# An attention and MLP kernel re-ordered by a list scheduler for all engines

## The chip, the cores and the metric

The kernel runs on one core of one Trainium2 chip. The metric is the device time of one execution in microseconds (us). Every kernel here was timed against the kernel before on the same chip, in turn; e1 to e4 ran on one chip, the later experiments on another, so experiments of different sets are best compared by their ratios to the kernel before. The profiled executions give a span, from the first to the last instruction, which is mostly about 1.7 us shorter than the time of the same execution. Executions are marked fast or slow; three slow ones (one of e1_hold, one of e7_resized, one of the kernel before in the rounds of e1 to e4) are left out of all ratios, but not out of the medians.

Engine names in the profile: PE is the matmul engine, PEld its weight load, DVE the vector engine, ACT the scalar engine, POOL is GpSimd, SP issues the DMAs.

## The reference

The program is the sum of a residual, a memory-augmented causal attention over four segments, and a SiLU MLP, all on one layer-normed input. S = 2048 rows, D = 512, 32 heads of 16, hidden size 1792, four segments of 512 rows.

```python
xn = layernorm(x)
# attention, per segment s and head
p     = softmax(qs @ ks.T * scale + causal_mask)
a_dot = p @ vs
a_mem = phi(qs) @ M / (phi(qs) @ z + 1e-6)
o     = g * a_mem + (1 - g) * a_dot
M, z  = M + phi(ks).T @ vs, z + phi(ks).sum()      # carried to the next segment
# sum
out = x + concat(o) @ wo + silu(xn @ w1) @ w2
```

## The kernel before

The heart of the kernel is a ring. Each segment has four blocks (dt) of eight heads, each block has five score tiles ("quads"), so there are 4 x 4 x 5 = 80 of them. A quad is a few matmuls into the PSUM tile `psS` (four banks, one buffer), one exp of 128x2048 elements on ACT into `Pt`, and a causal mask on POOL. There is one `psS`, so exp, next score matmul and next exp form a serial ring; I call the time from one exp's start to the next a turn. Everything else (projections q, k, v; the MLP's w1 and w2; the memory; normalisation; wo) is filled in between. It shares the other four PSUM banks, pool `pp`.

```python
ppool  = ctx.enter_context(tc.tile_pool(name="ppool", bufs=8))          # Pt
pp     = ctx.enter_context(tc.tile_pool(name="pp", bufs=4, space=PSUM)) # four banks
psatt  = ctx.enter_context(tc.tile_pool(name="psatt", bufs=1, space=PSUM))
ctx.enter_context(tc.manual_schedule(engines={ENG.PE}))   # only PE's order is the program's
...
def s_quad(st, dt, quad, tiles):
    psS = psatt.tile([P, 4, L], F32, name="psS")
    for par, kt, c in parts(quad):
        for g in range(4):
            nc.tensor.matmul(psS[:, g, c : c + nq], ...)   # four heads side by side
    Pt = ppool.tile([P, 4, L], BF16, name="Pt")
    nc.scalar.activation(out=Pt[:], in_=psS[:], func=AF.Exp, scale=SCALE)
    ...
    later(2000, masks)
```

PE's order comes from one loop: after each quad it fills about 1.5 us with generators (`due_fill`, `roll_fill`, `h_fill`), and at quad 1 of the next block it emits the block's PV, the product of the probabilities with V. PV makes two outputs, for even and odd heads, one bank each:

```python
if pend is not None and quad == 1:
    pv_part(*pend)
...
for par, dst in ((1, No_t), (0, N_t)):
    psPV = pp.tile([P, L], F32, name="psPV", tag="ps")     # one bank, filled and evacuated
    ...
```

The softmax sums of a segment are gathered by small DMAs into one tile `zf`, where ACT also writes the memory denominators; the tile is inverted, and spread again over 128 partitions by matmuls with a selection matrix. The output keeps one bank from the first w2 matmul to the last wo matmul:

```python
def replicate(ps, w, dt, rec):
    for b in range(2):
        nc.tensor.matmul(ps[:, 256*b : 256*b+256], lhsT=sel[:, b, w, dt, :], rhs=rec[:], ...)
...
w2_part(st, j, psO[:, :], ...)     # 14 matmuls, start at ft == 0
while st.get("normed", 0) < DT:    # the bank is held while normalisation is awaited
    yield
wo_part(s, st, j, psO[:, :], x_t)  # 4 matmuls, stop at the last
```

The softmax here doesn't subtract the row's maximum and nothing guards it: scores larger than these inputs give would overflow.

## Time and profile before

| | before |
|---|---|
| time, median of 5 runs (range) | 289.47 us (287.47 to 290.99) |
| profiled span | 288.9 us |
| first exp / last exp starts | 20.0 / 249.3 us |
| mean turn, (249.3 - 20.0) / 79 | 2.90 us |
| last exp's start to the end | 39.6 us |

Part 1 of the profile page of the kernel before gives, for each engine, busy time, share of the span and number of instructions.

```profile
span 288.9 us, 5119 instructions
PE 239.9 (83%) x1928; PEld 105.7 (37%) x1928; DVE 160.4 (56%) x280; ACT 203.0 (70%) x187; POOL 125.8 (44%) x222
```

No engine is full, so something serial must set the pace. The next view of the kernel before takes the exp's source line alone: count, shortest, median and longest duration in ns, first and last start, then what ACT sat idle for before it and who waited for it (us, times).

```profile
L484 ACT ACTIVATE Pt<-psS x80: 1856/1877/1933, 20.0 to 249.3; 128x2048 bf16<-128x2048 f32 x80
...
  PE psS L476: 19.3, 27
...
  PE psS L476: 21.0, 39
```

Eighty exps of 1.877 us are 150 us of a ring that lasts 231 us. The score matmul sometimes waits for the exp (21.0 us) and the exp sometimes for the score matmul (19.3 us): both sides of the ring are late in turn. The timeline of ACT in a quiet stretch of the kernel before shows how fast the ring can turn (start, duration, engine, line, operation, and in brackets the idle time before it with its releaser).

```profile
122.10 1.88 ACT L484 ACTIVATE Pt<-psS 128x2048 bf16<-128x2048 f32 x1
124.53 1.88 ACT L484 ACTIVATE Pt<-psS 128x2048 bf16<-128x2048 f32 x1 [0.56 <-PE psS L476]
127.14 1.88 ACT L484 ACTIVATE Pt<-psS 128x2048 bf16<-128x2048 f32 x1 [0.72 <-PE psS L476]
129.57 1.88 ACT L484 ACTIVATE Pt<-psS 128x2048 bf16<-128x2048 f32 x1 [0.56 <-PE psS L476]
```

These turns take 2.43 to 2.61 us, with 0.56 to 0.72 us of it the hand-over through PE. The mean of 2.90 us is therefore about 0.4 us above what the ring does when nothing is in its way. The end of the kernel before, in the timeline:

```profile
280.03 0.69 DVE L430 SCALAR_TENSOR_TENSOR o_t<-psO_3448,x_res 128x512 bf16<-128x512 f32 x1 [3.63 <-PE psO_3448 L424]
...
280.78 1.02 PE L424 MATMUL psO_3448<-wo_sb,oT 128*128 128x512 bf16 x4 [0.78 <-DVE o_t L430]
...
282.58 1.02 PE L424 MATMUL psO_3448<-wo_sb,oT 128*128 128x512 bf16 x4 [0.78 <-DVE o_t L430]
```

Each of the last three wo groups waits 0.78 us for the output operation of the group before it.

### The profile page before, as it was taken

To read this page: it belongs to the slowest core of one execution; us is meant where nothing else is said; L and a number is where in the kernel's file an instruction comes from. 1 tells how busy PE (TensorE), PEld (TensorE's weight loads), DVE (VectorE), ACT (ScalarE), POOL (GpSimd) and SP (SyncE) were. 2 spreads that over 40 slices of the span, in tenths; PEclk is the share of its full clock that TensorE was granted. 3 is DMA by queue.
4 is the path that set the end of the run, shared out by engine and by line. 5 is a ranking of instruction groups with operands and counts; after the bars stand their busy time and mean duration, and the time that the engine had idled before them with its cause. 6 is when DMAs were issued, how large, how long until landed. Compare 5 with 4: busy or idle time off the path is not lost.

```text
span 288.9 us, 5119 instructions
## 1 busy us (share of the span) xinstructions
PE 239.9 (83%) x1928; PEld 105.7 (37%) x1928; DVE 160.4 (56%) x280; ACT 203.0 (70%) x187; POOL 125.8 (44%) x222
## 2 busy tenths in 40 slices
PE   5277868877669885999998889699899999999983
PEld 5223324333223441334334343244353334444530
DVE  4439996666454746722157775652266533229722
ACT  1049868999938786877899789687768999714000
POOL 3807658566612468853334264844423334400000
PEclk9669979999989999899999999999999999999999
DMA  7998420101220011111201200001120010120003
GB/s 232 388 336 151 104 65 12 36 14 36 44 43 3 7 22 27 40 35 52 73 14 28 54 13 6 5 6 53 34 69 20 2 31 19 49 73 10 2 2 107
DMA packets 27065, 16.72 MB, mean 58 GB/s; under 512 B 15264, under 2 KB 26528, under 8 KB 27040
## 3 DMA queue, kind: packets, MB, share of 16 engines
q1 hardware_dynamic: 27040, 16.40, 21.0%
q8 instruction: 15, 0.25, 0.4%
q14 instruction: 10, 0.08, 0.1%
HBM read 9.96 MB, written 2.10 MB: 42 GB/s over the span
## 4 chain that ended last, share of the span: by engine, by line
PE 36%; ACT 23%; DVE 15%; issue 9%; DMA 7%; POOL 6%; SPq 2%; ACTq 0%; DVEq 0%
ACT Pt L484 18%; PE ps L188 12%; PE psO L415 7%; PE psS L476 4%; PE psO_3448 L415 4%; DMA xnT<-xn_t 3%; DMA x_in<-in_A_x_dram 2%; PE psO L424 2%; DVE qT L267 2%; ACT th L305 2%; POOL Pt L496 2%; DVE xn_t L143 2%; POOL ek L199 2%; DVE stats L132 2%; PE psPV L545 2%
## 5 line engine op out<-in xcount | busy, mean ns | idle before, releaser
L484 ACT ACTIVATE Pt<-psS 128x2048 bf16<-128x2048 f32 x80 | 150.2, 1877 | 21.9 <-PE psS L476 19.3
L496 POOL TENSOR_SCALAR_AFFINE_SELECT Pt<-Pt 128x512 bf16<-128x512 bf16 (+1 forms) x112 | 78.4, 714 | 103.0 <-ACT Pt L484 103.0
L188 PE MATMUL ps<-xnT,w_sb 128*128 128x512 bf16 x224 | 58.5, 392 | 4.9 <-DVE V_118 L273 2.3
L311 DVE SCALAR_TENSOR_TENSOR hT<-th,ps 128x512 bf16<-128x512 bf16 x56 | 37.8, 681 | 27.5 <-ACT th L305 27.1
L415 PE MATMUL psO<-w_sb,hT 128*128 128x512 bf16 x168 | 42.8, 386 | 0.0
L305 ACT ACTIVATE th<-ps 128x512 bf16<-128x512 f32 x56 | 33.5, 605 | 8.5 <-PE ps L188 5.1
L415 PEld LDWEIGHTS <-hT 128*128 128x128 bf16 x224 | 21.1, 99 | 24.8 <-issue 3.8
L476 PE MATMUL psS<-qT,kTo 32*128 32x512 bf16 (+3 forms) x256 | 17.7, 305 | 14.9 <-ACT Pt L484 13.5
L188 PEld LDWEIGHTS <-w_sb 128*128 128x128 bf16 x224 | 18.6, 99 | 30.8 <-issue 16.0
L476 PE MATMUL psS<-qT,kT 16*128 16x512 bf16 (+3 forms) x256 | 17.5, 302 | 7.7 <-ACT Pt L484 7.5
L430 DVE SCALAR_TENSOR_TENSOR o_t<-psO,x_res 128x512 bf16<-128x512 f32 x12 | 8.2, 687 | 27.5 <-PE psO L424 27.5
L476 PEld LDWEIGHTS <-kTo 32*128 32x128 bf16 x256 | 7.7, 92 | 34.9 <-issue 33.5
L199 POOL TENSOR_SCALAR ek<-ek 128x512 bf16<-128x512 bf16 x24 | 15.6, 650 | 7.9 <-ACT ek L196 7.8
L188 PE MATMUL ps<-xnT,wk_sb 128*128 128x512 bf16 x64 | 17.3, 395 | 1.4 <-DVE xn_t L143 0.7
L188 PE MATMUL ps<-xnT,wq_sb 128*128 128x512 bf16 x64 | 18.2, 411 | 0.0
L188 PE MATMUL ps<-wv_sb,xnT 128*128 128x512 bf16 x64 | 16.2, 390 | 1.3 <-DVE V_118 L273 1.2
L556 ACT CAST N_sb<-psPV 128x512 bf16<-128x512 f32 x16 | 9.4, 588 | 8.0 <-PE psPV L545 8.0
L132 DVE BATCH_NORM_STATS2 stats<-x_in 128x6 f32<-128x512 bf16 x16 | 10.4, 676 | 7.7 <-DMA x_in<-in_A_x_dram 7.7
L476 PEld LDWEIGHTS <-kT 16*128 16x128 bf16 x256 | 6.8, 92 | 20.7 <-issue 20.5
L267 DVE CAST qT<-ps 128x512 bf16<-128x512 f32 x16 | 11.0, 685 | 5.1 <-PE ps L188 5.1
L205 DVE SCALAR_TENSOR_TENSOR phiQT<-qT,ek 128x512 bf16<-128x512 bf16 x12 | 8.7, 724 | 9.0 <-POOL ek L199 9.0
L554 DVE CAST No_t<-psPV 128x512 bf16<-128x512 f32 x16 | 11.0, 687 | 4.7 <-PE psPV L545 4.7
(80 smaller groups left out, 273.1 us busy)
## 6 DMA issues: line engine op xcount, KB each, us to landing
w_sb<-in_B_w_dram SPq DMA_DIRECT2D x2, 1792.0 KB
x_in<-in_A_x_dram SPq DMA_DIRECT2D x8, 256.0 KB
x_res<-in_A_x_dram SPq DMA_DIRECT2D x16, 128.0 KB
out_dram<-o_t SPq DMA_DIRECT2D x16, 128.0 KB
N_sb<-No_t SPq DMA_DIRECT2D x64, 16.0 KB
wk_sb<-in_A_wk_dram SPq DMA_DIRECT2D x1, 512.0 KB
wq_sb<-in_A_wq_dram SPq DMA_DIRECT2D x1, 512.0 KB
wv_sb<-in_A_wv_dram SPq DMA_DIRECT2D x1, 512.0 KB
```

The costliest lines, as they stand in the source:

```text
L132: nc.vector.bn_stats(out=stats[:], in_=xts[(s, 2 * half + j)])
L188: nc.tensor.matmul(ps[:, :], lhsT=lhsTs(ki), rhs=rhss(ki), start=(ki == 0), stop=(ki == DT - 1))
L199: nc.gpsimd.tensor_scalar(out=ek[:], in0=ek[:], scalar1=1.0, scalar2=0.0, op0=ALU.min, op1=ALU.max)
L267: nc.vector.tensor_copy(out=st["qT"][:, dt, :], in_=ps[:, :])
L305: nc.scalar.activation(out=th[:], in_=ps[:, :], func=AF.Tanh, scale=0.5)
L311: nc.vector.scalar_tensor_tensor(out=hT[:], in0=th[:], scalar=1.0, in1=ps[:, :], op0=ALU.add, op1=ALU.mult)
L415: nc.tensor.matmul(psO, lhsT=st["hT"][ft][:, j * P : (j + 1) * P], rhs=w2_sb[:, ft, :], start=(ft == 0), stop=False,)
L476: nc.tensor.matmul(psS[:, g, c : c + nq], lhsT=kk[r0:r1, dt, kt * P : (kt + 1) * P], rhs=st["qT"][r0:r1, dt, kt * P : L], start=True, stop ...
L484: nc.scalar.activation(out=Pt[:], in_=psS[:], func=AF.Exp, scale=SCALE)
L496: nc.gpsimd.affine_select(out=v, in_=v, compare_op=ALU.is_ge, fill=0.0, base=0, pattern=[[0, v.shape[1]], [1, P]], channel_multiplier=-1,)
L554: nc.vector.tensor_copy(out=dst[:], in_=psPV[:, :])
L556: nc.scalar.copy(out=dst[:], in_=psPV[:, :])
```

## The change

The generators go. The whole program becomes a graph of operations, each with an engine, an occupancy and a latency in ns (a duration model), a due time, and the PSUM banks that it takes and frees. A greedy list scheduler orders all five instruction streams; the emission follows its order exactly, since every engine's order is now the program's. Along with it: x is loaded once and kept in SBUF; buffers become rings per block; the reciprocals are written to DRAM and read back replicated instead of being spread by matmuls; w2 and wo get separate accumulation groups with an SBUF partial sum `xa` between them; N casts, kT copies and the `zf` add move from ACT to DVE.

The diff, cut to its core:

```diff
-    ctx.enter_context(tc.manual_schedule(engines={ENG.PE}))
+    ctx.enter_context(tc.manual_schedule())
...
+RING = dict(xnT=2, kT=6, kTo=6, qT=6, ..., Pt=8, ..., rep=6, ..., psS=1, drec=4, ...)
+NB = 4
...
+            pvo = op("PE", 1090, 215, pv, tau(n0 + 8), r=keys + ..., w=[("PV", s, dt)],
+                     take=list(tk), mode="C", kind="PV")      # tk: TWO banks at once
...
+            op("DVE", 300, 130, norm, base + 2000 + 700 * j, ...)   # a duration of the model
...
-    def replicate(ps, w, dt, rec):      # matmuls with sel
+                def rep(K, dt=dt, w=w, slot=slot):
+                    d = K.drec[s][1 - w, 8 * dt : 8 * dt + 8, :]
+                    src = bass.AP(tensor=d.tensor, offset=d.offset, ap=[[L, 8], [0, 16], [1, L]])
+                    K.nc.sync.dma_start(out=K.rep[slot][:], in_=src)
...
+        split = True                    # w2 into xa, wo in a group of its own
...
+    def schedule(self):
+        while left:
+            best = None
+            for e in engs:
+                cand = None
+                for o in ready[e]:
+                    t = max(free[e], est[o.n])
+                    if o.take:
+                        av = sorted(b for b in banks)
+                        need = av[len(o.take) - 1]     # a PV needs the second-earliest bank
+                        t = max(t, need)
+                        if o.kind == "w1" and pend >= 2:
+                            t = INF
+                    ...
+                    slack = {"S": 110, "exp": 200}.get(o.kind, 0)
+                    key = -1e9 if o.kind in ("S",) else o.due
+                    ...
+                    if key < ck:
+                        if t - slack <= ct:            # urgent, but only if it starts as early
+                            cand = (t, key, slack, o)
+                    elif t < ct - cs:                  # else: the earlier start wins
+                        cand = (t, key, slack, o)
+                if cand and (best is None or cand[0] < best[0]):
+                    best = cand
```

## The prediction

> **What bounds it now.** The span is 288.9 us. No engine is full (page, part 1: PE 83%, ACT 70%, DVE 56%, POOL 44%), but a serial ring is long. The 80 exps of 128x2048 (80 x 1.88 us on ACT) share one PSUM tile, psS: exp, next score matmul, next exp. In the timeline its shortest turns are 2.41 to 2.61 us. The first exp starts at 20.0, the last at 249.3: 2.90 us a turn (by tens 3.1, 3.1, 3.4, 2.6, 2.8, 2.8, 2.8). The excess is order: in the waits view PE waits 21 us on exp for psS and ACT 19.3 us on score matmuls; the chain of waits at 100 to 120 us walks through POOL kTo and ek, DVE evacuations and ACT ek in turn. After the last exp 39 us follow: PV, seven left-over w1 groups, normalisation interleaved with w2, and four wo groups of which three wait 0.78 us for the output op before.
>
> PE's real occupancy: 512-column matmuls follow each other at 0.216 us. About 716 of them (155 us), 80 score quads at 0.43 (35), 16 PVs at 1.25 (20), rest 6: 216 us, after a first projection at 15.2 us. [...] 0.39 reported, 0.216 start to start.
>
> **What changes.**
> - Every engine's order, not PE's alone, comes from a list schedule, score matmuls first. This attacks the excess over about 2.5 us a turn: 79 x 0.35 to 0.45 = 28 to 36 us, on the critical path.
> - ACT loses 16 N casts (9.4), kT copies (2.3), zf (1.4): 13 us. DVE takes them, plus 16 w2 evacuations into xa (11): about 170 us, not binding.
> - 56 replication matmuls leave PE (6 us), and their tiles the four banks. In exchange a DRAM write and a replicated read, about 2 to 2.5 us each as the trace's small DMAs take; off the path except in the last segment. pq and a_t, reading SBUF only, should fall from 0.68 to about 0.4 us.
> - w2 apart from wo: no bank is held through normalisation; the last segment's w2 is done early.
> - x stays in SBUF: 16 reloads (2 MB) go; DMA was not binding.
>
> **Sum.** First exp stays near 20. 79 turns at 2.5 to 2.6 put the last at 218 to 226. Then a latency chain: mask and PV 2.5, evacuations 1.4, sums DMA 3.2, reciprocal 2, DRAM write and read 6.5, pq, psN, oT, four wo, output, store 10: about 26 us. Total 244 to 252, plus a little because a fixed order mis-times what the model mis-sizes: **251 us**, 8 in 10 within **241 to 267**. Chances: faster by over 2% 0.93, within 2% 0.04, slower 0.03.
>
> **What would show it.** Right: exps from about 20 to 222, mean turn below 2.65; ACT busy about 190; small PE waits on exp; last exp to end under 32 us, with DMA in its chain; wo four in a row. Wrong: turns still 2.8 or more, with ACT or PE waiting on DVE or POOL at the head of a fixed queue; x_all, one tile, serialising outputs against stores; a tail over 35 us from DMA hops.
>
> **What would make it wrong.** In-order engines block on an op the model put too early (DMA waits above all: zf sums, transposes, the DRAM hop), and one late op stops unrelated ones; SP's queue, about 0.5 us an issue, is in order too. POOL masks may come late for PV. If PE saturates, 216 us plus head and tail is the floor.

A last exp at 218 to 226 and a tail of about 26 us make 244 to 252, and 251 us was forecast. The DRAM write and read (2 to 2.5 us each, 6.5 in the sum) are an estimate from before's small DMAs: its chain of waits has 1.53 and 1.56 us for `zf` and 2.29 us for `N_sb`, after issues of 0.5 to 0.6 us; in after's tail the two took 5.81 us. `pq` and `a_t` took 0.68 us in before, with a PSUM operand, and a median of 0.42 us in after, from SBUF only.

## The result, and the profile after

| | before | after |
|---|---|---|
| time, median of 5 runs (range) | 289.47 us (287.47 to 290.99) | 277.84 us (275.94 to 278.57) |
| ratio of fast runs (95% interval) | 1 | 0.9599 (0.9539 to 0.966) |
| profiled span | 288.9 us | 274.2 us |
| first exp / last exp starts | 20.0 / 249.3 us | 14.15 / 244.46 us |
| mean turn | 2.90 us | 2.915 us |
| last exp's start to the end | 39.6 us | 29.7 us |

A ratio is the mean time of one kernel's fast runs over the mean of the other's fast runs of the same rounds, so it is not quite the ratio of the medians printed here.

The kernel is faster, but by 4%, not by the predicted 13%, and outside the range on record. The span fell by 14.7 us: 5.9 at the head, 9.9 in the tail, and the ring in between lasted 1.0 us longer than before (230.3 against 229.3). What the change was mainly for, the ring, gained nothing. These pieces are of one execution each. The one of after was the fastest of its five (275.94 us), which is why the spans differ by 14.7 us and the median times by 11.6.

Part 1 of the profile page after, in the same columns as before:

```profile
span 274.2 us, 4983 instructions
PE 228.6 (83%) x1857; PEld 97.7 (36%) x1888; DVE 177.2 (65%) x309; ACT 193.1 (70%) x164; POOL 124.0 (45%) x213
```

Work did move: ACT fell by 9.9 us (13 were costed), DVE rose by 16.8. The exp's line after (eight groups, since the ring has eight named buffers; two shown, then what ACT waited for before its exps and what the score matmuls waited for):

```profile
L488 ACT ACTIVATE Pt__129<-psS x10: 1858/1877/1878, 14.2 to 227.1; 128x2048 bf16<-128x2048 f32 x10
...
L488 ACT ACTIVATE Pt__136<-psS x10: 1877/1877/1907, 34.7 to 244.5; 128x2048 bf16<-128x2048 f32 x10
...
  PE psS L477: 29.5, 39
  PE psb__196 L515: 1.8, 1
  PE psb__194 L515: 1.7, 1
...
  PE psS L477: 9.5, 11
```

An exp lasts 1.877 us as before. PE now waits less for exps (9.5 us instead of 21.0) and ACT waits more for score matmuls (29.5 instead of 19.3). Two exps waited for a PV matmul (L515), which is new. Looking for the first of them in the timeline after:

```profile
28.45 1.09 POOL L502 TENSOR_SCALAR_AFFINE_SELECT Pt__133<-Pt__133 128x1024 bf16<-128x1024 bf16 x1
...
34.71 1.88 ACT L488 ACTIVATE Pt__136<-psS 128x2048 bf16<-128x2048 f32 x1 [1.04 <-PE psS L477]
...
37.61 1.02 PE L148 MATMUL psb__194<-xnT__89,w 128*128 128x512 bf16 x4
...
42.48 1.03 PE L148 MATMUL psb__197<-xnT__90,wq 128*128 128x512 bf16 x4
...
47.44 0.38 PE L148 MATMUL psb__195<-w,hT__137 128*128 128x512 bf16 x1
...
49.91 0.40 PE L515 MATMUL psb__194<-Pt__129,V__123 128*32 128x512 bf16 x4
...
50.36 1.88 ACT L488 ACTIVATE Pt__129<-psS 128x2048 bf16<-128x2048 f32 x1 [1.69 <-PE psb__194 L515]
```

Exp 7 (counting from 0) starts at 34.71 and exp 8 at 50.36: one turn of 15.65 us. Exp 8 writes `Pt__129`, the buffer of exp 0, which the PV of block 0 has to read first. The last input of that PV, the mask of `Pt__133`, was ready at 29.54, and yet the PV starts at 49.91. PE was idle for only 1.9 of these 20 us (1.52 of them in one wait that ended at 33.31): it ran w1, q, k, v and w2 groups. The bracket names only the last 1.69 us of idleness, because ACT had small work (tanh, exp for phi) before it; a reader who goes by the waits view alone misses this gap. The same stretch in windows of the kernel after (columns: stretch and its length; busy us and count of PE, PEld, DVE, ACT, POOL; granted TensorE clock; DMA share; GB/s):

```profile
20.00:35.00 15.00, 11.02 (x71) 3.85 (x70) 13.24 (x27) 11.02 (x11) 9.56 (x16) 1.00 0.69 126
35.00:50.00 15.00, 14.74 (x76) 6.28 (x79) 13.64 (x28) 10.41 (x18) 7.94 (x14) 1.00 0.18 36
50.00:120.00 70.00, 66.04 (x594) 28.45 (x604) 49.03 (x83) 62.75 (x56) 39.74 (x59) 1.00 0.18 35
```

PE and DVE look full in the stretch 35 to 50 (14.74 and 13.64 of 15 us), and ACT well used (10.41), although the ring stands still. PE does useful work there, but the wrong work.

The tail after, in the timeline:

```profile
254.11 0.35 DVE L641 TENSOR_SCALAR rec__173<-rec,gcol 128x256 bf16<-128x256 f32 x1
...
260.27 0.42 DVE L683 TENSOR_TENSOR pq__181<-phiQ__112,rep__176 128x512 bf16<-128x512 bf16 x1 [5.81 <-DMA rep__176<-drec__201]
260.75 0.58 PE L148 MATMUL psb__196<-pq__181,Mbf__190 128*128 128x512 bf16 x1 [12.10 <-DVE pq__181 L683]
...
265.75 0.63 PE L148 MATMUL psb__196<-wo,oT__166 128*128 128x512 bf16 x1
...
266.18 0.63 PE L148 MATMUL psb__196<-wo,oT__167 128*128 128x512 bf16 x1
...
268.90 0.38 PE L148 MATMUL psb__194<-wo,oT__166 128*128 128x512 bf16 x1
```

The tail is a latency chain now: from the reciprocals at 254.46 to the first product `pq` at 260.27 pass 5.81 us of DRAM write and read. PE waits 12.10 us, and its first back-to-back matmuls after that, from 265.75, follow each other at 0.43 us instead of 0.216; the granted clock was 0.50 from 253 to 265.37 and 0.52 from 265.37 to 268.7. The full rate is back at about 268.7 (granted clock 1.00 from there to 274), some 3.3 us after PE had come near to continuous work (265.37). The product `pq`, which now reads SBUF only, takes 0.42 to 0.43 us in this tail, where DVE's tensor-by-tensor operations with a PSUM operand take 0.67 to 0.69 in the same trace (`oT`), and `pq` itself took 0.68 in before, with a PSUM operand.

### The profile page after: what moved, and what is told of

Same layout as the page of the kernel before. It is cut to its first block, busy times and chain, and to the rows that moved or that the text cites. A ratio compares the mean times of both kernels' runs of the same rounds, so it can differ in the third digit from the quotient of the medians.

```text
span 274.2 us, 4983 instructions
## 1 busy us (share of the span) xinstructions
PE 228.6 (83%) x1857; PEld 97.7 (36%) x1888; DVE 177.2 (65%) x309; ACT 193.1 (70%) x164; POOL 124.0 (45%) x213
## 3 DMA queue, kind: packets, MB, share of 16 engines
HBM read 11.53 MB, written 2.33 MB: 51 GB/s over the span
## 4 chain that ended last, share of the span: by engine, by line
PE 47%; DVE 15%; ACT 13%; DMA 10%; issue 8%; SPq 4%; POOL 2%; DVEq 0%; ACTq 0%; POOLq 0%
PE psb__197 L148 11%; PE psb__195 L148 10%; PE psb__194 L148 8%; PE psb__196 L148 7%; PE psS L477 6%; ACT Pt__129 L488 3%; DMA wv<-in_A_wv_dram 3%; DMA x_all<-in_A_x_dram 2%; PE psb__196 L515 2%; ACT th__158 L434 1%; PE psb__197 L515 1%; ACT Pt__134 L488 1%; PE psb__194 L515 1%; DVE rec L640 1%; DMA rep__176<-drec__201 1%
## 5 line engine op out<-in xcount | busy, mean ns | idle before, releaser
L148 PEld LDWEIGHTS <-w 128*128 128x128 bf16 x224 | 21.4, 99 | 32.2 <-issue 11.5
L488 ACT ACTIVATE Pt__129<-psS 128x2048 bf16<-128x2048 f32 x10 | 18.8, 1875 | 6.7 <-PE psS L477 3.6
L488 ACT ACTIVATE Pt__134<-psS 128x2048 bf16<-128x2048 f32 x10 | 18.8, 1877 | 6.6 <-PE psS L477 4.6
L488 ACT ACTIVATE Pt__136<-psS 128x2048 bf16<-128x2048 f32 x10 | 18.8, 1880 | 5.8 <-PE psS L477 5.0
L488 ACT ACTIVATE Pt__133<-psS 128x2048 bf16<-128x2048 f32 x10 | 18.8, 1879 | 5.1 <-PE psS L477 4.2
L488 ACT ACTIVATE Pt__135<-psS 128x2048 bf16<-128x2048 f32 x10 | 18.8, 1875 | 3.7 <-PE psS L477 3.5
L488 ACT ACTIVATE Pt__131<-psS 128x2048 bf16<-128x2048 f32 x10 | 18.8, 1879 | 3.5 <-PE psS L477 3.3
L488 ACT ACTIVATE Pt__132<-psS 128x2048 bf16<-128x2048 f32 x10 | 18.8, 1877 | 3.2 <-PE psS L477 3.1
L488 ACT ACTIVATE Pt__130<-psS 128x2048 bf16<-128x2048 f32 x10 | 18.8, 1877 | 2.4 <-PE psS L477 2.2
L502 POOL TENSOR_SCALAR_AFFINE_SELECT Pt__129<-Pt__129 128x512 bf16<-128x512 bf16 (+1 forms) x14 | 10.7, 780 | 13.9 <-ACT Pt__129 L488 13.9
L502 POOL TENSOR_SCALAR_AFFINE_SELECT Pt__133<-Pt__133 128x512 bf16<-128x512 bf16 (+1 forms) x14 | 10.2, 746 | 11.9 <-ACT Pt__133 L488 11.9
L502 POOL TENSOR_SCALAR_AFFINE_SELECT Pt__136<-Pt__136 128x512 bf16<-128x512 bf16 (+1 forms) x14 | 9.6, 702 | 12.9 <-ACT Pt__136 L488 12.9
L502 POOL TENSOR_SCALAR_AFFINE_SELECT Pt__132<-Pt__132 128x512 bf16<-128x512 bf16 (+1 forms) x14 | 10.4, 759 | 10.7 <-ACT Pt__132 L488 10.7
L502 POOL TENSOR_SCALAR_AFFINE_SELECT Pt__135<-Pt__135 128x512 bf16<-128x512 bf16 (+1 forms) x14 | 10.0, 724 | 11.4 <-ACT Pt__135 L488 11.4
L502 POOL TENSOR_SCALAR_AFFINE_SELECT Pt__131<-Pt__131 128x512 bf16<-128x512 bf16 (+1 forms) x14 | 9.6, 701 | 10.4 <-ACT Pt__131 L488 10.4
L502 POOL TENSOR_SCALAR_AFFINE_SELECT Pt__134<-Pt__134 128x512 bf16<-128x512 bf16 (+1 forms) x14 | 9.8, 714 | 8.6 <-ACT Pt__134 L488 8.6
L502 POOL TENSOR_SCALAR_AFFINE_SELECT Pt__130<-Pt__130 128x512 bf16<-128x512 bf16 (+1 forms) x14 | 9.7, 707 | 8.5 <-ACT Pt__130 L488 8.5
L148 PE MATMUL psb__196<-xnT__89,w 128*128 128x512 bf16 x36 | 9.6, 379 | 4.0 <-DVE hT__139 L440 2.1
L148 PE MATMUL psb__196<-pq__181,Mbf__190 128*128 128x512 bf16 x2 | 1.2, 608 | 12.1 <-DVE pq__181 L683 12.1
L148 PEld LDWEIGHTS <-wk 128*128 128x128 bf16 x80 | 7.4, 98 | 10.5 <-issue 3.6
L148 PEld LDWEIGHTS <-wq 128*128 128x128 bf16 x80 | 7.2, 97 | 9.6 <-issue 2.7
L148 PE MATMUL psb__194<-xnT__90,w 128*128 128x512 bf16 x36 | 10.3, 408 | 0.0
```

The lines of the kernel that those rows point to most:

```text
L148: K.nc.tensor.matmul(K.bank(t)[:, 0:ncol], lhsT=lhsT(K, i), rhs=rhs(K, i), start=(i == 0), stop=(i == n - 1),)
L488: K.nc.scalar.activation(out=K.Pt[n % RING["Pt"]][:], in_=K.psS[:], func=AF.Exp, scale=SCALE)
L502: K.nc.gpsimd.affine_select(out=a, in_=a, compare_op=ALU.is_ge, fill=0.0, base=0, pattern=[[0, a.shape[1]], [1, P]], channel_multiplier=-1,)
```

## The experiments

My theory (A) was starvation by bank count. PV asks for two banks at one moment, all other groups for one. The scheduler takes the operation that can start earliest, and a more urgent one displaces it only if it can start as early. With four banks in constant use, the second-earliest free bank always comes after the earliest, so a one-bank group always starts earlier than PV. PV waits until the one-bank work runs dry, and with it the ring, which has only eight `Pt` buffers for blocks of five. The scheduler writes its planned start times down, and they can be read without a chip: planned exp 7 and 8 are at 30.0 and 46.3 us, and the first PV, whose inputs the plan has ready at 26.1, is placed at 45.0. So the gap is in the plan, and the chip carried it out. The plan's span is 262.2 us, the chip's 274.2. (The schedule was computed again, without a chip. If the test lets a PV start when one bank is free, exp 8 is planned at 32.5 us. If instead a rule that is cut from the diff above goes, which delays a PV by 0.7 us before its due time, exp 8 stays at 46.3. So in the plan it is the test for two banks that makes the gap.)

The rivals were that the moved work slows the ring (DVE's load, the DRAM hop, w2 apart from wo), and that the fixed order of in-order engines does so, by blocking on operations that the model mis-times. The expectations below name the theories by letters; each states its own, and A is the same throughout the first five runs.

| kernel | first exp | last exp | mean turn | last exp to end | span | time, median | ratio to before (95%) |
|---|---|---|---|---|---|---|---|
| before | 20.0 | 249.3 | 2.90 | 39.6 | 288.9 | 289.47 | 1 |
| after | 14.15 | 244.46 | 2.915 | 29.7 | 274.2 | 277.84 | 0.9599 (0.9539, 0.966) |
| e1_hold | 13.96 | 224.57 | 2.666 | 31.0 | 255.6 | 257.19 | 0.8847 (0.8766, 0.8928) |
| e2_joint | 13.96 | 256.11 | 3.065 | 41.4 | 297.5 | 300.05 | 1.0372 (1.0279, 1.0464) |
| e3_joint_hold | 14.24 | 228.10 | 2.707 | 46.9 | 275.0 | 278.83 | 0.9616 (0.952, 0.9712) |
| e4_tailpe | 14.10 | 229.28 | 2.724 | 29.0 | 258.3 | 258.55 | 0.8917 (0.8838, 0.8996) |
| e5_peonly | 23.42 | 273.05 | 3.160 | 30.4 | 303.5 | 306.04 | 1.0536 (1.0484, 1.0588) |
| b1_late_x | 17.49 | 249.03 | 2.931 | 39.6 | 288.6 | 290.3 | 1.0007 (0.9976, 1.0038) |
| e6_lesspe | 14.37 | 223.27 | 2.644 | 29.6 | 252.9 | 256.06 | 0.8824 (0.8789, 0.886) |
| e7_resized | 16.63 | 219.97 | 2.574 | 32.0 | 252.0 | 253.44 | 0.8717 (0.8668, 0.8767) |
| e8_vlate | 13.29 | 219.36 | 2.608 | 31.0 | 250.4 | 252.31 | 0.872 (0.8685, 0.8755) |
| e9_vlate_tailpe | 13.40 | 218.91 | 2.601 | 27.9 | 246.8 | 248.5 | 0.8582 (0.8553, 0.861) |
| e10_tuned | 13.35 | 222.09 | 2.642 | 27.7 | 249.8 | 251.56 | 0.8688 (0.866, 0.8716) |

Starts and turns are read from the traces, in us. All results matched the reference within its tolerance, e6_lesspe too, which is wrong, so this check did not see the matmuls left out.

### e1_hold: banks are held for a PV that is due

When a PV is ready and due, another operation may take a bank only if that leaves two for the PV, that is, if three are free by then (`av` is the sorted list of the times at which the banks come free).

```diff
                         if o.kind == "w1" and pend >= 2:
                             t = INF
+                        if o.kind != "PV" and t < INF:
+                            due_pv = [x for x in ready["PE"] if x.kind == "PV" and est[x.n] <= t and x.due <= t]
+                            if due_pv and av[2] > t:
+                                t = INF
```

> The one edit: while an overdue PV block waits for its two PSUM banks, no other group may take a bank if that would leave fewer than two. Theory A (the list schedule starves PV of two banks at once; the stall of exp 7 to 8, 15.6 us in the trace, is written into the order itself): the stall shrinks to under 7 us, the last exp comes near 226 instead of 244.5, the time near 260 us (256 to 264). Rival B (PE was busy with needed work during the stall, so the work only moves): the stall goes but the other turns lengthen; time 273 to 279 us. Rival C (the in-order engines mis-time, whatever the order says): the time falls by less than half of the 18 us by which the plan's own end falls (262.2 to 244.0).

Measured: 257.19 us (255.22 to 259.25), 20.6 us less than after. The timeline of e1_hold at the same place:

```profile
34.17 1.88 ACT L488 ACTIVATE Pt__136<-psS 128x2048 bf16<-128x2048 f32 x1 [1.04 <-PE psS L477]
...
37.66 0.40 PE L515 MATMUL psb__196<-Pt__129,V__123 128*32 128x512 bf16 x4 [0.41 <-DVE hT__143 L440]
...
38.64 1.88 ACT L488 ACTIVATE Pt__129<-psS 128x2048 bf16<-128x2048 f32 x1
```

The turn from exp 7 to exp 8 fell from 15.65 to 4.47 us. That is 11.2 of the 19.7 us that the ring lost; the remaining 8.5 are spread over the other 78 turns (2.75 to 2.64 us on average). The plans fit this: in the plan of after, six of the later PVs stand 4 to 9 us behind their inputs (for example placed at 139.0, ready at 129.9) and all stand behind their due times; in the plan of e1_hold no PV after the third is more than about 3 us behind its inputs. A part of the 8.5 may be the TensorE clock: in after it was granted at 0.50 from 215 to 220 us and 0.65 from 220 to 226, while over its whole ring e1_hold had 0.99; what this cost was not measured. Theory A is confirmed. Its rivals are refuted as the main cause: B expected 273 to 279 us and C a fall of less than half of 18 us, and with the moved work and the fixed order of engines unchanged in kind the time fell by 20.6 us and the ring turns in 2.666 us.

### e2_joint and e3_joint_hold: w2 and wo in one group again, without and with the hold

```diff
-        split = True
+        split = False
```

> Undoes one part of the change: w2 and wo of a token block are again one accumulation group of 18 matmuls in one bank (the flag for it is in the code), nothing else. Theory A (banks decide): a group of 18 that waits for normalisation holds a bank much longer, PV starves more, plan 281.2 instead of 262.2; the time is 290 to 300 us, with a stall before exp 8 near 21 us and another near exp 53. Rival B (PE's work decides): 16 output evacuations less on DVE and the same PE work; time 273 to 282 us.

> The joint w2 and wo group together with the bank hold of the first run of this set. Theory A: plan 260.8; time 272 to 280 us, stall before exp 8 below 7 us; splitting w2 from wo is then worth 14 to 20 us by itself, mostly at the end (last exp as in the first run, the tail longer by about 15 us since w2 of the last segment sits behind normalisation or holds all banks). Rival B: same as the first run of this set within 5 us.

Measured: e2_joint 300.05 us, e3_joint_hold 278.83. The joint group holds a bank through normalisation, which makes the second bank rarer. In e2_joint the stall before exp 8 grew, as the timeline of ACT shows:

```profile
33.86 1.88 ACT L488 ACTIVATE Pt__136<-psS 128x2048 bf16<-128x2048 f32 x1 [1.04 <-PE psS L477]
55.26 1.86 ACT L488 ACTIVATE Pt__129<-psS 128x2048 bf16<-128x2048 f32 x1
```

That is 21.4 us for one turn. So w2 apart from wo did not cause the stall, it eased it. With the hold, the difference between split and joint is 278.83 - 257.19 = 21.6 us, a little over what I had expected. Most of it lies in the tail, 46.9 against 31.0 us after the last exp. In e3_joint_hold PE waits 12.17 us, until 248.95, and runs w2 of the last segment only from 254.12; in e1_hold, where w2 keeps no bank, it starts at 224.39, before that segment is normalised.

### e4_tailpe: the DRAM hop of the last segment undone, on top of e1_hold

```diff
+        onpe = s == NSEG - 1
+        if not onpe:
             op("SP", 1500 if s else 500, 2100, wr, ...)         # write of rec to DRAM
+        if onpe:                                                # two matmuls per tile instead
+            K.nc.tensor.matmul(K.bank(tk)[:, 256*b : 256*b+256],
+                               lhsT=K.sel[:, w, b, dt, :], rhs=K.rec[i2][:], ...)
```

> Bank hold as in the first run, and in the last segment alone the reciprocals are replicated by selection matmuls on PE as before the change, not through DRAM. Theory D (the DRAM hop costs the tail): from the reciprocal's end to the first pq the trace showed 5.8 us of DVE waiting; matmuls need about 1; last exp to end falls from about 30 to 24 to 26 us, time 3 to 6 us under the first run. Rival E (the tail is bound by the chain of DVE, PE and output after it, and PSUM operands make pq and a_t 0.68 instead of 0.42 us): within 2 us of the first run.

Measured: 258.55 us, 1.4 us more than e1_hold, with overlapping intervals of the ratio, so no difference is shown. The run is confounded, because adding operations makes the greedy scheduler choose another order everywhere: the last exp came at 229.28 instead of 224.57. In the tail itself the way from the start of the reciprocal to the end of the last `oT` fell from 14.8 to 10.5 us, but the reciprocal began 5.2 us after the start of the last evacuation (239.22 against 234.06) where e1_hold took 3.6 (232.92 against 229.34), queued behind an `xa` operation on DVE that waited 2.33 us for PE. And from 248.13 to 253.56 its wo matmuls followed each other at 0.43 us, with the granted clock at 0.50. So the hop cost about 4.3 us where it stood, and the experiment didn't show whether removing it pays. That was tried again in e9_vlate_tailpe.

### e5_peonly: after's PE program, the other engines' order left to the framework

As in the kernel before, only PE's order is the program's. PE's program is identical to that of after.

```diff
-    ctx.enter_context(tc.manual_schedule())
+    ctx.enter_context(tc.manual_schedule(engines={mybir.EngineType.PE}))
```

> The changed kernel with the planned order kept on PE alone; the other engines are ordered by the framework, as in the kernel before. PE's program is the same, 182 rows of DVE's, some 40 of ACT's and 30 of POOL's move. Theory A (the changed kernel's time is set by PE's order, with its starved PV, and not by the order of the other engines): 275 to 282 us, stall before exp 8 still 14 to 17 us. Rival F (the order of all engines is what gave the 4%): 286 us or more, first exp back near 20.

Measured: 306.04 us, 28 us more than after and 5% more than before. My expectation was wrong: I had thought the stall alone made the time and the order of the other engines worth little. The first cost is at the head, in the timeline of e5_peonly:

```profile
15.35 0.69 DVE L277 BATCH_NORM_STATS2 stats__85<-x_all 128x6 f32<-128x512 bf16 x1 [5.79 <-DMA x_all<-in_A_x_dram]
15.96 0.67 DVE L322 CAST xnT__89<-psb__196 128x512 bf16<-128x512 f32 x1
...
16.78 1.86 PE L148 MATMUL psb__195<-xnT__89,wk 128*128 128x512 bf16 x4 [5.67 <-DMA bcol<-in_A_beta_dram]
```

DVE has the statistics of segment 1 at the head of its queue and waits 5.79 us for their load, while the evacuation of segment 0's transposed x, which PE needs, stands behind them. (The releaser named for PE is only the last of several; what PE needed is the cast just before it.) The first exp comes at 23.4 instead of 14.15, the stall at exp 8 is still there (43.52 to 59.20), and the mean turn is 3.16 us. So the planned order of the other engines is worth 28 us with this PE program, which was planned together with it; what it is worth with another PE program this doesn't say. The kernel before carries a similar wait (4.18 us of DVE on a load at 10.59); I asked next whether it costs anything there. The converse, a program's order for DVE or for all engines in the kernel before, could not be built for all engines: with the emission order taken literally, the check before the chip reports a deadlock. So that corner stays untested.

### b1_late_x: the kernel before, with segment 1's first load behind the weights

```diff
-    load_x(1, 0)
     for dst, src in ((w1_sb, B_w1), (wo_sb, A_wo), (w2_sb, B_w2)):
         nc.sync.dma_start(out=dst[:], in_=src.rearrange("(ko ki) n -> ki ko n", ki=P))
+    load_x(1, 0)
     load_x(1, 1)
```

> The kernel before with one load moved: the first half of x of segment 1 is loaded after w1, wo and w2, so that its statistics no longer stand in DVE's queue ahead of the first normalisations. Theory G (the 5.9 us by which the first exp came earlier after the change is this head-of-queue wait of DVE, 4.2 us in the trace, plus POOL memsets ahead of the first power): first exp at 16 to 18.5 instead of 20.0, and the time 1 to 4 us under before. Rival H (the head was gained by something else: x ring, fewer loads): first exp stays at 19.5 to 20.5.

Measured: 290.3 us, ratio 1.0007: the same time. The first exp did move, from 20.0 to 17.49. By exp 10 the gain was gone (52.55, against 51.06 in before). The head is not on the path of the kernel before: the exps that follow wait for other things. My expectation was right about the first exp and wrong about the time.

### e6_lesspe: e1_hold with 48 matmuls of w2 left out (wrong)

```diff
+                if name == "w2" and i in (3, 7, 11):
+                    return
```

> Wrong result on purpose: the bank-hold version in its exact order, but 3 of the 14 w2 matmuls of each token block are not emitted: 48 matmuls of 0.216 us, 10.4 us of PE. Theory I (once the stall is gone PE is the bound: 18 to 20 of 20 us busy in most stretches): 7 to 10 us under the bank-hold version (257.2), so 247 to 250. Rival J (the ring of exp and score matmul, or order, sets the pace): under 4 us, so 253 to 258.

Measured: 256.06 us, 1.1 us less than e1_hold, for 48 x 0.216 = 10.4 us less PE work. The two were run on different chips, and the intervals of their ratios overlap. PE is 90% busy on the page of e1_hold, and taking this work from it gained next to nothing. That fits rival J, ring or order; the run doesn't tell these two apart. The prediction's floor ("If PE saturates, 216 us plus head and tail is the floor") is none: with the head and tail of e1_hold it would be 216 + 14.0 + 31.0 = 261 us, and e1_hold's span is 255.6, since some of PE's work lies in the head and the tail.

### e7_resized: e1_hold with durations taken from the trace

I compared start-to-start times on DVE and POOL in the trace with the model's occupancies, and set the ones that were off to their measured means.

```diff
-            op("DVE", 662, 150, stats, ...      ->  805
-            op("POOL", 770, 150, rstd, ...      ->  960
-            op("DVE", 300, 130, norm, ...       ->  490
-            op("POOL", 655, 130, odd, ...       ->  750
-        op("DVE", 690 if acc else 605, 140, st  ->  790 / 705
-                op("DVE", 340, 135, a0, ...     ->  560
-            op("DVE", 340, 135, pq / at, ...    ->  435 / 460
-        op("DVE", 1900, 150, rc, ...            ->  2070
```

> The bank-hold version planned with DVE and POOL durations as the trace has them (statistics 0.81 instead of 0.66, normalisation 0.49 for 0.30, pq and a_t 0.44 to 0.46 for 0.34, phi 0.10 more, reciprocal 2.07 for 1.90, POOL kTo and power longer). Plan 247.1 instead of 244.0. Theory C (the 11.6 us between plan and trace in the bank-hold run are order gone wrong through mis-sized ops): trace minus plan falls to 7 or less and the time to 250 to 255. Rival K (the difference is work and clock that no order removes): 256 to 261.

Measured: 253.44 us, 3.7 us less than e1_hold, on another chip; the intervals of the two ratios just touch (0.8766 and 0.8767), so the gain is likely but small. The mean turn is 2.574, inside the predicted 2.5 to 2.6, in part by luck: the first exp came 2.7 us later than in e1_hold, which shortens the ring, and with the first exp back the mean turn is 2.608 (e8_vlate). The plan is now 4.9 us short of the chip (247.1 against 252.0) instead of 11.6 in e1_hold (244.0 against 255.6). Part of what the model missed is not the operation's own time. The layer-norm scaling has, in the view of its source line in after:

```profile
L296 DVE TENSOR_SCALAR xn__88<-x_all,mv,rstd x8: 394/400/1240, 7.2 to 132.0; 128x512 bf16<-128x512 bf16 x8
```

Its median is 0.40 us and its longest 1.24 us; that longest one, in the timeline of after, started in the same moment as a POOL mask that ran for 1.09 us:

```profile
28.45 1.24 DVE L296 TENSOR_SCALAR xn__88<-x_all,mv,rstd 128x512 bf16<-128x512 bf16 x1
28.45 1.09 POOL L502 TENSOR_SCALAR_AFFINE_SELECT Pt__133<-Pt__133 128x1024 bf16<-128x1024 bf16 x1
```

This is a coincidence of two operations, and another one went differently: the same operation at 48.60 began while POOL was at work (48.27 to 48.88, as far as POOL's times can be trusted) and took 0.42 us. No run here tests whether POOL's work is what lengthens DVE's. A duration model with one number per operation can hold the mean of this and not the case.

### e8_vlate, e9_vlate_tailpe, e10_tuned: towards the best version

In e7_resized the first exp had slipped from 13.96 to 16.63, because a v group of segment 0 was placed ahead of the first k and q. e8_vlate lets v groups of segment 0 start no earlier than 13 us in the plan. e9_vlate_tailpe adds e4's edit for the last segment. e10_tuned changes two of the scheduler's constants.

```diff
 e8:  +            nb=13000 if s == 0 else 0,        # not_before of the first v matmul
 e9:  + e4's edit, the selection matrix built after 60 us
 e10: -T0 = 12500                                     +T0 = 11500
      -slack = {"S": 110, "exp": 200}                 +slack = {"S": 160, "exp": 200}
```

> The resized version with one more edit: the V projections of segment 0 may not start before 13 us, since in the resized run they stood ahead of the first k and q and the first exp came at 16.6 instead of 14.0. Plan 247.2 (resized 247.1). Theory L (the head is on the path once the rest flows): first exp at 14.0 to 14.6 and the time 1 to 3 us under the resized version (253.4). Rival M (as in the kernel before, where a first exp 2.5 us earlier gained nothing): 252.5 to 255.

> The previous kernel of this set plus the last segment's reciprocals replicated by matmuls instead of through DRAM; unlike in the first try the order before the tail is kept (same planned start of the last exp, 212.4; plan 242.7 against 247.2). Theory D2 (the first try lost in the middle what it saved in the tail): time 3.5 to 5.5 us under the previous kernel; last exp at the same time within 0.7 us; last exp to end 26 to 28 us instead of 31. Rival E: within 1.5 us of it.

> The previous kernel with two numbers of the scheduler changed after trying 160 combinations on the plan alone (origin of the due dates 11.5 us instead of 12.5, slack by which a score matmul may jump the queue 160 ns instead of 110). Plan 239.7 against 242.7. If the plan's differences of 3 us are real on the chip: 2 to 4 us under the previous kernel, 243 to 247 us. If they are within what the plan cannot see (trace minus plan was 4.9 to 11.6): no different, 246 to 251.

Measured: 252.31, 248.5 (248.22 to 249.18) and 251.56 us. e8_vlate moved the first exp by 3.3 us (13.29) and left the ratio as it was (0.872 against 0.8717); at exp 10 the two kernels stand at 42.76 and 42.82. The head isn't on the path here either. e9_vlate_tailpe gained 3.8 us over e8_vlate with its last exp at nearly the same time (218.91 against 219.36); 27.9 us are left after it instead of 31.0. Here the experiment of e4 is clean, and leaving out the DRAM hop of the last segment is worth 3 to 4 us. With the hop, in e8_vlate, wo ran at 0.43 us a matmul from 242.12 to about 244.3, and the mean granted clock was 0.986 against 0.998 in e9_vlate_tailpe; how much of the gain this makes was not measured. The tail of e9_vlate_tailpe in the timeline:

```profile
230.19 0.35 DVE L656 TENSOR_SCALAR rec__174<-rec,gcol 128x256 bf16<-128x256 f32 x1
...
232.34 0.69 DVE L711 TENSOR_TENSOR pq__182<-phiQ__113,psb__198 128x512 bf16<-128x512 bf16 x1 [0.82 <-PE psb__198 L683]
...
240.26 0.39 PE L148 MATMUL psb__198<-wo,oT__170 128*128 128x512 bf16 x1 [0.99 <-DVE oT__170 L733]
240.48 0.38 PE L148 MATMUL psb__197<-wo,oT__167 128*128 128x512 bf16 x1
```

`pq` starts 1.8 us after the reciprocals, not 5.81, though it reads PSUM and takes 0.69 us. PE has w2 work left until then and never idles for more than 0.99 us, and wo runs at 0.216 us from its start. e10_tuned had the shortest plan of all (239.7 us, against 242.7 for e9) and ran 3 us longer than e9: a difference of 3 us between these two plans said nothing about the chip. e9_vlate_tailpe is the best kernel, 14% below before and 11% below after.

## Why the prediction was wrong

The step that failed is, as it was put, "79 turns at 2.5 to 2.6 put the last at 218 to 226". The ring took 230.3 us where 79 x 2.55 = 201 us were expected. The other two terms, "First exp stays near 20" and a tail of "about 26 us", were off by -5.9 and +3.7, so the ring's +28.9 us is more than the whole miss of 26.8 (277.84 against 251); that the other two terms cancel in part is luck. What failed is the assumption that the scheduler's order keeps every turn near 2.5: it let PV, which needs two banks, starve, and one turn alone took 15.65 us. The runs account for most of it: banks held for PV took the ring from 230.3 to 210.6 us (e1_hold). Measured durations took it to 203.3 (e7_resized), of which 2.7 us is only the later first exp; the last exp moved by 4.6 (224.57 to 219.97). With the first exp back the ring is 206.1 us (e8_vlate), 4.6 above the expected figure, and these are not explained.

- "Every engine's order, not PE's alone, comes from a list schedule, score matmuls first. This attacks the excess": right that order is the matter (e5_peonly: 28 us for the order of the other engines, with this PE program). Wrong that this scheduler's order has no excess of its own. Its text was in the diff: PV takes two banks, and a one-bank operation with an earlier start beats a more urgent one. I priced the operations and did not follow the choice rule through one block.
- "plus a little because a fixed order mis-times what the model mis-sizes": the mechanism fits, and was worth about 3.7 us in time (e7_resized, with intervals that just touch). It was the smaller of the two.
- "Wrong: turns still 2.8 or more, with ACT or PE waiting on DVE or POOL at the head of a fixed queue": the turns were 2.915, but for another reason. ACT waited for a PV that PE had been given no banks for, and PE was busy almost all the while.
- "First exp stays near 20": it came at 14.15; an earlier first exp was worth nothing in the two kernels where it was tried alone (b1_late_x, e8_vlate), and in after itself it was not tried.
- The tail, "about 26 us": measured 29.7, with the DRAM hop in its chain and the wo groups in a row, as described. Matmuls at 0.43 us instead of 0.216, after a wait of 12.10 us, add to it.
- ACT's loss ("13 us", "ACT busy about 190") and DVE's gain ("about 170 us, not binding") were roughly right: 193.1 us, a loss of 9.9, and 177.2. The SBUF-only products (`pq`, `a_t`) fell from 0.68 to a median of 0.42 us (0.41 to 1.22), as costed. `x_all` as one tile did not serialise stores and outputs: the waits view of after names no store as what an output operation waited for.
- "PE's real occupancy" by 0.216 us a matmul was useful in showing that PE had room; e6_lesspe fits it.
- "w2 apart from wo: no bank is held through normalisation; the last segment's w2 is done early": right, and worth more than I had expected in e3_joint_hold (14 to 20): 21.6 us with the hold (e3_joint_hold against e1_hold), and 22.2 without it (e2_joint against after), there with a longer stall in it.

What stays open: how much a program's order for all engines would give the kernel before with its own PE order (it could not be built), why single DVE operations took 1.24 and 1.64 us where 0.40 and about 0.68 are common, and how the 11.6 us that the change did gain divide among its parts; only w2 apart from wo was undone by itself.

## What to carry to other kernels

When a program is ordered by a greedy scheduler, an operation that needs two of a scarce resource at once can starve behind those that need one, unless something is held back for it; follow the choice rule through one round of the critical ring, or look at the planned starts for the longest gap, before pricing operations. A gap in the ring can hide behind busy engines, so plot the spacing of the ring's own instruction rather than waits or busy shares. And before crediting a gain at the head, see whether a later step of the ring (exp 10 here) still has it.

## What the runs show of busy shares, the clock and DVE beside POOL

- Busy shares: ACT was 70% busy in after and PE 83%. But the same operations in another order gained 20.6 us (e1_hold) with ACT's work as it was (193.1 and 192.2 us), and 10.4 us less work on PE gained 1.1 us (e6_lesspe). The shares did not point to what the order of a serial ring cost.
- The clock: after the 12.10 us wait in after's tail matmuls followed each other at 0.43 us, with 0.50 granted. In e1_hold a lower clock came after an idle gap of 2.32 us before 110.14, in a stretch in which PE had been little used before it (0.82 of 3 us from 107 to 110). In e4_tailpe the clock fell to 0.50 at about 247.1 though PE, 66% busy from 243 to 247, had idled for at most 0.22 us at a time in the 4 us before, while in e9_vlate_tailpe the wo matmuls after a gap of 0.99 us started 0.22 us apart (240.26 and 240.48). No run tested what lowers the clock. The windows of e1_hold (columns as above) show the granted clock at 0.60 just after its gap:

```profile
107.00:110.00 3.00, 0.82 (x10) 0.23 (x10) 2.93 (x7) 2.37 (x2) 1.08 (x4) 1.00 0.34 69
110.00:114.00 4.00, 3.86 (x14) 1.20 (x14) 4.00 (x7) 3.00 (x4) 3.78 (x5) 0.60 0.22 48
```

- DVE beside POOL: single DVE operations took 1.24 us instead of 0.40 (after, 28.45) and 1.64 instead of about 0.68 (e1_hold, 112.27, a two-input operation beside a POOL product of 1.18 us from 112.17); that POOL is the reason is not shown. Modelling mean durations gained 3.7 us (e7_resized).
